# One fused adaLN block on one core: contractions over 448 rows as 64-row pairs of two tiles, stage 1 evicted by tile pairs, LayerNorm 2's scale and shift on transposed blocks

## The chip, the core and the metric

The kernel runs on one NeuronCore of one Trainium2 chip. The core has five engines with instruction queues of their own: TensorE (PE, matmuls; its weight loads are listed as PEld), VectorE (DVE), ScalarE (ACT), GpSimd (POOL) and SyncE (SP), which here issues most transfers. The metric is device time in microseconds (us) of the launch, the median of several runs; lower is better.

## The reference

One block with two branches on x of 2048 x 448 (bf16), a linear attention with learned softmax features (16 heads of 28) and a gated MLP with a spatial mixing matrix of 2048 x 2048. `silu(c) @ w_mod` gives two shifts, two scales and two gates.

```
sa, ca, ga, sb, cb, gb = split(silu(c) @ w_mod)
h = layernorm(x) * (1 + ca) + sa
q, k, v = heads(h @ wqkv)
phi(t) = concat(softmax(t @ w_phi), softmax(-t @ w_phi))
kv = phi(k)^T v;  z = sum(phi(k));  o = phi(q) kv / (phi(q) z + 1e-6)
x = x + ga * (o @ wo)
h = layernorm(x) * (1 + cb) + sb
z1, z2 = split(gelu(h @ w_in));  z2 = layernorm(z2)
g = w_sp @ z2 + b_sp[:, None]
x = x + gb * ((z1 * g) @ w_out)
```

Here w_in is 448 x 1792, so z1 and z2 have 896 columns.

## The kernel before

The 2048 rows are 16 tiles of 128. The work is a set of small steps (nested functions of `fast_path`), each of which issues a few instructions for one tile, one pair of tiles or one block. One string, `ORDER`, lists the steps; a word is `step:arguments/engine@bank`. The loop over its words is the program: every engine runs its instructions in that order, and each instruction waits only for the data and buffers that it needs. DMAs stand in the queue of the engine after the slash (`/Y` is SP); the transposes through the DMA (`T1`, `T2`, `T3`, and `W` for w_sp) always stand in SP's queue.

The steps fall into three stages.

Stage 1 (k, v and features). `l1s`, `l1e`, `l1r`, `l1a` normalise x without scale and shift; these are folded into the weights. Tiles are transposed in 4 blocks of 112 of the 448 columns (`hT`). Per tile `kM` and `vM` (L893, L901) are 4 matmuls each; `kE`, `kF` take exp of k and of -k on ACT, `vC` copies v on ACT, `kS` sums and `kR` inverts on DVE, `kP` multiplies on DVE or POOL, `kA` (L922) adds 8 narrow matmuls into the sum kv.

Stage 2 (q, attention output, LayerNorm 2, z). `qM` (L945) makes q for four tiles in one half of the heads. Per tile `nM` (L973) makes numerators and denominators, 8 matmuls of 120 columns over 128 rows against a block-diagonal kv; `nX`, `nC`, `nS` make the weights of the two softmax halves, `nT` (L989, DVE, 896 elements) applies them, `nA` (L995) adds the halves into `opad`. `T2` transposes it to `oT`. `wM` (L1005) multiplies by wo with 4 matmuls, for some tiles with a fifth that adds x (L1003). `wR` (L1010, L1012) adds the residual and sums the rows, `wQ` sums the squares, `l2R` and `l2r` make mean and inverse deviation, `l2a` (L1038) normalises into `xpad`, and `T3` transposes it to `hT`, in the same 4 blocks of 112 rows; a row of ones beside them carries the shift. Scale and shift of LayerNorm 2 are folded into w_in by `SCw` (L797 to L801), `SHw` (L784) and `FB` (L790). `zM` (L1049) makes z2 for a tile with 8 matmuls of 448 columns, `zG` applies GELU, `zQ`, `zR`, `zW`, `zN` normalise to `f_z2n`. `yM` (L1078) makes a 128-column block of z1, transposed, for four tiles with 4 matmuls of 512 columns, and `yG` applies GELU.

Stage 3 (mixing and output). The product with w_sp is done with 7 block products for each 2 x 2 (`P`, L1124, 8 matmuls of 512 columns each; `tT` and `sS` make the sums that they need), with column block 6 apart (`gM`, L1145). `d` and `x` add b_sp and multiply by z1; `oM` (L1159) multiplies by w_out with 7 matmuls, `oE` (L1162) adds x, `oD` stores.

PSUM has three slots of two banks (A0 to A2) and two of one (B0, B1) in stages 1 and 2.

```
for word in ORDER.split():
    ...
        STEPS[nm](*[int(v) for v in arg.split(",") if v], **kw)
```

Of the kernel before, what the change touches and what calls it, by code (L numbers as in the profile page):

```python
# [1266 lines left out]
```

## Time and profile before

| | us |
|---|---|
| median of 3 runs | 249.34 |
| lowest and highest | 248.21, 249.86 |
| the profiled execution, whole | 249.99 |
| its span in the trace | 248.1 |
| stage 1 and what leads to it, to the first nM | 54.0 |
| stage 2, to the first matmul of the mixing that runs in a row | 84.4 |
| mixing and output, to the last matmul | 105.3 |
| last residual add and store | 4.4 |

The busy shares of the 40 slices of the span, from the page:

```profile
PE   8999999989999899999999999999999999999992
DVE  5689999978998889687571997798976363645552
ACT  2488898846999697867897100000000000000000
POOL 4768997500587468988508000521129610124430
PEclk9999999999999999999999999999999999999999
```

Each digit is the busy share of an engine in one 6.2 us slice, in tenths; PEclk is the clock that TensorE was granted, full throughout. A matmul's row shows its whole passage (352 ns for 448 columns), though the next one follows long before its end; so PE's busy share says that it always has something under way, not that it is at its peak. ACT ends after slice 23, where the mixing begins.

### The profile page before, as it was taken

To read this page: it belongs to the slowest core of one execution; us is meant where nothing else is said; L and a number is where in the kernel's file an instruction comes from. 1 tells how busy PE (TensorE), PEld (TensorE's weight loads), DVE (VectorE), ACT (ScalarE), POOL (GpSimd) and SP (SyncE) were. 2 spreads that over 40 slices of the span, in tenths; PEclk is the share of its full clock that TensorE was granted. 3 is DMA by queue.
4 is the path that set the end of the run, shared out by engine and by line. 5 is a ranking of instruction groups with operands and counts; after the bars stand their busy time and mean duration, and the time that the engine had idled before them with its cause. 6 is when DMAs were issued, how large, how long until landed. Compare 5 with 4: busy or idle time off the path is not lost.

```text
span 248.1 us, 4186 instructions
## 1 busy us (share of the span) xinstructions
...
## 2 busy tenths in 40 slices
PE   8999999989999899999999999999999999999992
...
DVE  5689999978998889687571997798976363645552
ACT  2488898846999697867897100000000000000000
POOL 4768997500587468988508000521129610124430
PEclk9999999999999999999999999999999999999999
...
GB/s 176 265 245 106 188 86 161 208 160 144 45 79 114 137 121 145 157 154 180 190 171 0 152 176 186 0 1 0 3 0 37 0 0 3 56 0 37 21 95 65
DMA packets 68207, 25.22 MB, mean 102 GB/s; under 512 B 58129, under 2 KB 67602, under 8 KB 68178
## 3 DMA queue, kind: packets, MB, share of 16 engines
...
q8 instruction: 14, 0.23, 0.4%
q14 instruction: 15, 0.12, 0.2%
...
## 4 chain that ended last, share of the span: by engine, by line
PE 59%; DVE 13%; POOL 12%; issue 8%; ACT 3%; DMA 3%; POOLq 0%; DVEq 0%
PE g_ps L1124 29%; PE o_ps L1159 9%; PE z_ps L1049 5%; PE g_ps L1145 5%; DVE f_ksum L907 4%; PE z_ps L1078 4%; DMA f_hT<-f_xpad 3%; DVE f_st L859 3%; PE warm_ps L729 3%; POOL f_xpad L1038 2%; POOL f_ar L995 2%; POOL f_phik L914 1%; DVE f_phik L914 1%; POOL f_zv L1035 1%; DVE f_kr L911 1%
## 5 line engine op out<-in xcount | busy, mean ns | idle before, releaser
L1133 DVE TENSOR_TENSOR f_zb<-g_ps,f_zb 128x512 f32<-128x512 f32 (+1 forms) x31 | 20.5, 670 | 17.1 <-PE g_ps L1124 16.7
L1124 PEld LDWEIGHTS <-f_z2n 128*128 128x128 bf16 x192 | 18.8, 98 | 22.7 <-issue 0.3
L1140 POOL TENSOR_TENSOR f_z1T<-f_zb,f_z1T 128x512 bf16<-128x512 f32 (+1 forms) x11 | 11.9, 1101 | 33.6 <-DVE f_zb L1133 33.6
L1078 PE MATMUL z_ps<-f_hT,f_ar 112*128 112x512 bf16 x112 | 26.1, 379 | 1.3 <-DMA f_hT<-f_xpad 1.3
L1049 PE MATMUL z_ps<-f_ar,f_hT 112*128 112x448 bf16 (+1 forms) x128 | 26.7, 352 | 0.0
L1140 POOL TENSOR_TENSOR f_z1T<-f_Sx,f_z1T 128x512 bf16<-128x512 f32 x6 | 8.0, 1333 | 39.3 <-DVE f_Sx L1133 39.3
L1159 PE MATMUL o_ps<-f_wout,f_z1T 128*128 128x448 bf16 x112 | 22.5, 352 | 0.0
L1124 PE MATMUL g_ps<-f_ar 128*128 128x512 bf16 x94 | 22.2, 379 | 0.1
L1081 ACT ACTIVATE f_z1T<-z_ps,f_zb 128x512 bf16<-128x512 f32 x28 | 18.2, 684 | 6.7 <-PE z_ps L1078 6.5
L950 ACT ACTIVATE f_Eq<-q_ps 128x1024 bf16<-128x1024 f32 x16 | 16.4, 1033 | 5.8 <-PE q_ps L945 5.8
L1049 PEld LDWEIGHTS <-f_hT 112*128 112x128 bf16 (+1 forms) x128 | 12.2, 97 | 11.6
L1078 PEld LDWEIGHTS <-f_ar 112*128 112x128 bf16 x112 | 10.9, 98 | 14.1 <-issue 1.6
L989 DVE TENSOR_TENSOR f_ar<-num,f_w 128x896 bf16<-128x896 f32 x16 | 17.0, 1086 | 0.4
L896 ACT ACTIVATE f_E<-k_ps 128x448 bf16<-128x448 f32 x32 | 15.7, 563 | 3.1 <-PE k_ps L893 1.6
L907 DVE TENSOR_REDUCE f_ksum<-f_E 128x32 f32<-128x896 bf16 x16 | 16.7, 1060 | 0.2 <-ACT f_E L896 0.2
L1053 ACT ACTIVATE f_zb<-z_ps 128x896 bf16<-128x896 f32 x16 | 14.6, 913 | 4.2 <-PE z_ps L1049 3.8
L1124 PE MATMUL g_ps<-f_Eq,f_z2n 128*128 128x512 bf16 x70 | 16.2, 379 | 0.1
L1159 PEld LDWEIGHTS <-f_z1T 128*128 128x128 bf16 x112 | 11.0, 98 | 10.7
L1162 DVE TENSOR_TENSOR f_xpad<-o_ps,f_x 128x448 bf16<-128x448 f32 x16 | 9.9, 622 | 8.0 <-PE o_ps L1159 7.9
L945 PE MATMUL q_ps<-f_hT,f_Wq 113*128 113x512 bf16 (+1 forms) x64 | 15.0, 378 | 0.4 <-ACT f_Eq L950 0.4
L1124 PEld LDWEIGHTS <-f_ar 128*128 128x128 bf16 x96 | 9.4, 98 | 11.1 <-DVE f_ar L1102 0.2
L893 PE MATMUL k_ps<-f_Wk,f_hT 113*128 113x448 bf16 (+1 forms) x64 | 14.2, 352 | 0.2 <-ACT f_E L896 0.2
...
## 6 DMA issues: line engine op xcount, KB each, us to landing
...
```

Of the source, the lines that this page charges most:

```text
L896: nc.scalar.activation(out=Er[i % NR][:, :, s, :], in_=ps["k" + str(i)][:, 0, 0:D].rearrange("p (a e) -> p a e", a=8), func=ACT.Exp, scale ...
L907: nc.vector.tensor_reduce(out=ksum[:, i], in_=Er[i % NR][:].rearrange("p a s (f h) -> p (a s) h f", h=2), axis=AX.X, op=ALU.add)
L945: nc.tensor.matmul(t[:, u, :], lhsT=Wq[0:KR[m], m, cc * P:(cc + 1) * P], rhs=hT[0:KR[m], 4 * st:4 * st + 4, m, :], start=(m == 0), stop=(m ...
L950: nc.scalar.activation(out=Eq[st // 2][:, 2 * c2:2 * c2 + 2, s, (st % 2) * 512:(st % 2 + 1) * 512], in_=ps["q" + str(n)][:], func=ACT.Exp, ...
L989: nc.vector.tensor_tensor(out=tr[i % 2][:], in0=numv(i)[:, :, :, 0:DH], in1=wr[i // 2 % 2][:, i % 2].unsqueeze(3).to_broadcast([P, 2, H, D ...
L1049: nc.tensor.matmul(t[:, hf, 0:D], lhsT=hT[0:KR[m], i, m, :], rhs=win_s[0:KR[m], m, FH + hf * D:FH + (hf + 1) * D], start=(m == 0), stop=(m ...
L1078: nc.tensor.matmul(t[:, 0, :], lhsT=win_s[0:CB, m, fc * P:(fc + 1) * P], rhs=hT[0:CB, 4 * st:4 * st + 4, m, :], start=(m == 0), stop=(m == ...
L1081: nc.scalar.activation(out=stage_b()["z1T"][:, fc, st * 512:(st + 1) * 512], in_=ps["y%d_%d" % (st, fc)][:, 0, :], func=ACT.Gelu_apprx_tan ...
L1124: nc.tensor.matmul(g, lhsT=sta[:, m, :], rhs=mov[:, m, :], start=(m == 0 and i in (1, 6, 7)), stop=(m == 7), skip_group_check=True)
L1133: nc.vector.tensor_tensor(out=o, in0=x, in1=y, op=ALU.add)
L1140: eng.tensor_tensor(out=z, in0=T[r][:, c0:c1], in1=z, op=ALU.mult)
L1159: nc.tensor.matmul(ps["o" + str(t)][:, 0, 0:D], lhsT=later["z1T"][:, FO[n], t * P:(t + 1) * P], rhs=wout_s[:, FO[n], :], start=(n == 0), s ...
```

## The change

Pairs of half height. 448 is 7 x 64. Where a contraction ran over 4 blocks of 112 rows, it now runs over 7 blocks of 64. Tile 2j stands on rows 0 to 63 and tile 2j + 1 on rows 64 to 127 of one 128-row block, and the weights (wo, w_in) are in SBUF twice, once on each half. A matmul of the lower half is issued right behind that of the upper half, into another PSUM bank. So `wM`, `zM` and `yM` handle two tiles (`yM` eight), and the transposes `T2` and `T3` move 7 blocks a pair instead of 8. `nM` splits its 128-row contraction in the same way into two of 56 rows: 16 matmuls of 60 columns instead of 8 of 120.

```diff
+    def zM(j, sa, sb):
+        t = [bank(sa), bank(sb)]
...
+        for hf in range(2):
+            for cc in range(7):
+                for a in range(2):
+                    nc.tensor.matmul(t[a][:, hf, 0:D], lhsT=hT2[64 * a:64 * a + 64, j, cc, :], rhs=W2[64 * a:64 * a + 64, cc, hf * D:(hf + 1) * D],
+                                     start=(cc == 0), stop=(cc == 6))
-        for m in range(KC):
-            nc.tensor.matmul(t[:, 0, :], lhsT=win_s[0:CB, m, fc * P:(fc + 1) * P], rhs=hT[0:CB, 4 * st:4 * st + 4, m, :], start=(m == 0), stop=(m == KC - 1))
+        for cc in range(7):
+            for a in range(2):
+                nc.tensor.matmul(t[:, a, :], lhsT=W1[64 * a:64 * a + 64, cc, fc * P:(fc + 1) * P], rhs=hT2[64 * a:64 * a + 64, 4 * u:4 * u + 4, cc, :],
+                                 start=(cc == 0), stop=(cc == 6))
-        for cc in range(KC):
-            nc.tensor.matmul(t[:, 0, 0:D], lhsT=oT[0:CB, i % 4, cc, :], rhs=wo_s[0:CB, cc, :], start=(cc == 0 and not with_x), stop=(cc == KC - 1))
+        for cc in range(7):
+            for a in range(2):
+                nc.tensor.matmul(t[:, a, 0:D], lhsT=oT[64 * a:64 * a + 64, j % 2, cc, :], rhs=wo2[64 * a:64 * a + 64, cc, :], start=(cc == 0), stop=(cc == 6))
-                nc.tensor.matmul(t[:, s, cc * 120:(cc + 1) * 120], lhsT=E[:, cc, s, o:o + P],
-                                 rhs=KVbd[:, s, cc, :, :].rearrange("p h d -> p (h d)"), start=True, stop=True)
+                for a in range(2):
+                    nc.tensor.matmul(t[:, a, (s * 4 + cc) * 60:(s * 4 + cc + 1) * 60], lhsT=E[64 * a:64 * a + 56, cc, s, o:o + P],
+                                     rhs=KVd[64 * a:64 * a + 56, s, cc, :, :].rearrange("p h d -> p (h d)"), start=True, stop=True)
```

LayerNorm 2's scale and shift are no longer in w_in. `SCw`, `SHw` and `FB` go; the four columns are made by `cB` and `eB`, and a new step `hS` multiplies and adds in place on a transposed block, for two pairs at a time (256 columns), 28 instructions on ACT, DVE and POOL.

```diff
+    def hS(cc, a, b, eng):
+        v = hT2[:, a:b, cc, :]
+        if eng is nc.scalar:
+            nc.scalar.activation(out=v, in_=v, func=ACT.Identity, scale=colB[:, 1, cc:cc + 1], bias=colB[:, 0, cc:cc + 1])
+        else:
+            eng.tensor_scalar(out=v, in0=v, scalar1=colB[:, 1, cc:cc + 1], scalar2=colB[:, 0, cc:cc + 1], op0=ALU.mult, op1=ALU.add)
```

Stage 1 by pairs. k and v of two tiles go to the two banks of one slot, so that `kE`, `kF`, `vC`, `kS` and `kR` are one instruction for two tiles. `yG` covers 1024 columns instead of 512, `nA` two tiles instead of one. `wR` is always on DVE with the residual added there.

```diff
-        nc.vector.tensor_reduce(out=ksum[:, i], in_=Er[i % NR][:].rearrange("p a s (f h) -> p (a s) h f", h=2), axis=AX.X, op=ALU.add)
+        nc.vector.tensor_reduce(out=ksum[:, 2 * j:2 * j + 2], in_=Er[j % 3].rearrange("p t a s (f h) -> p (t a s) h f", h=2), axis=AX.X, op=ALU.add)
-        eng.tensor_tensor(out=opad[:, i % NO, :, 0:CB], in0=v[0], in1=v[1], op=ALU.add)
+        eng.tensor_tensor(out=opad[:, j % 2].rearrange("p c t e -> p c t e"), in0=v[0], in1=v[1], op=ALU.add)
```

The moments of both later LayerNorms are split into single steps `mA` to `mF`, which the order may place on DVE or POOL one by one. PSUM is one tile of eight banks with four slots of two, and most SBUF buffers lie in one arena.

All steps stand in a new order. Of the string, one line of each:

```diff
-nX:0 nX:1 qF:3 nC:0 csB@B0 W:0,1 ld:win1/Y nC:1 nS:0 ccB@B1 nT:0 qM:4@A2 qE:4 nA:0/V nT:1 ecB nA:1/V wos:3/V qM:5@A1 nM:2@A0 qF:4 esB nX:2 nM:3@A2 nX:3
+nX:1/S nC:1 nD:0 ld:w21/S du:2@B7 qM:3@A3 nI:0 nW:0 nT:0 qE:2 nT:1 qF:2 nM:2@A1 qF:3 nM:3@A2 nX:2/S qM:4@A0 wos:4,7/G nX:3/S nC:3 nA:0/G W:0,7 nC:2 nD:1 nI:1
```

Two places of the order. First POOL's queue in stage 2, ahead of the first normalised tile of LayerNorm 2. Before (f_m and f_v are mean and inverse deviation, f_cb the scale, f_ar the arena):

```order
L799 TENSOR_SCALAR f_ar<-f_ar,f_cb_82 112x896
L995 TENSOR_TENSOR f_ar<-f_ar 128x4x112
L1025 TENSOR_SCALAR f_m_89<-f_s_87 128x2
L1026 TENSOR_TENSOR f_sq<-f_m_89 128x2
L1028 TENSOR_SCALAR f_v_90<-f_s_88 128x2
L1029 TENSOR_TENSOR f_v_90<-f_v_90,f_sq 128x2
L1032 TENSOR_SCALAR f_v_90<-f_v_90 128x2
L1035 TENSOR_TENSOR f_v_90<-f_v_90,f_mhalf 128x2
L1038 TENSOR_SCALAR f_xpad<-f_x,f_m_89,f_v_90 128x4x112
```

and with the change, from the mean of tiles 0 and 1 on:

```order
L1016 TENSOR_SCALAR f_m_82<-f_s_80 128x2
L1036 TENSOR_TENSOR f_v_83<-f_v_83,f_mhalf 128x2
L1039 TENSOR_SCALAR f_xpad<-f_x,f_m_82,f_v_83 128x7x64 x2
L1020 TENSOR_TENSOR f_sq<-f_m_82 128x2
L988 TENSOR_TENSOR f_ar<-f_ar 128x2x7x64
L1028 TENSOR_TENSOR f_v_83<-f_v_83,f_sq 128x2
L1032 TENSOR_SCALAR f_v_83<-f_v_83 128x2
```

The power and the two normalisations of tiles 2 and 3 now come first; between the mean and the deviation of tiles 0 and 1 stands an add of a whole pair into `opad`, and the power and the normalisation of tiles 0 and 1 follow behind the last row.

Second SP's queue at the same time, around the first transposes of stage 2. Before:

```order
L644 DMA f_ar<-in_B_w_in_dram 112x2x1792
L875 DMA_TRANSPOSE f_ar<-f_ar 128x4x128 x2
L875 DMA_TRANSPOSE f_ar<-f_ar 128x8x128 x2
L1043 DMA_TRANSPOSE f_hT<-f_xpad 128x4x128
L875 DMA_TRANSPOSE f_ar<-f_ar 128x8x128
```

and with the change:

```order
L670 DMA f_ar<-in_w_mod_dram 112x4x960
L991 DMA_TRANSPOSE f_ar<-f_ar 128x7x128 x2
L675 DMA f_ar<-in_B_w_in_dram 64x7x896
L991 DMA_TRANSPOSE f_ar<-f_ar 128x7x128
L1043 DMA_TRANSPOSE f_hT<-f_xpad 128x7x128 x2
```

The first transpose of LayerNorm 2 (L1043) came as a single tile behind two single tiles and two pairs of `opad`; now it comes as two pairs in a row behind five pairs, with two loads of weights among those.

More of the change, by code (lines that the diff above doesn't have):

```diff
@@ L637, in fast_path @@
-    later = {}
+    crr = [persist.tile([P, 2, 2, 2, 8], F32, name=f"f_cr{r}") for r in range(2)]
+    dnr = [persist.tile([P, 4, 8], F32, name=f"f_dn{r}") for r in range(2)]
+    wr = [persist.tile([P, 4, 2, 8], F32, name=f"f_w{r}") for r in range(2)]
+    g_rep1 = persist.tile([P, D], BF, name="f_g_rep")
+    bmask = persist.tile([CB, 4], BF, name="f_bmask")
+    one1 = persist.tile([1, 1], BF, name="f_one1")
+    e = persist.tile([DC, KC], F32, name="f_e")
+    scol = persist.tile([DC, KC], BF, name="f_scol")
@@ L639, in fast_path @@
+    zero = carve(51072, 512)
+    c_row = carve(51584, D)[0:1]
+    ot = [xflat[:, 512 * r:512 * r + D] for r in range(4)]
+    g_rep = [g_rep0, g_rep1[:]]
     xv = A_x[0].rearrange("(n p) d -> p n d", p=P)
@@ L786, in FB, with ecA @@
-    def FB(slot):
-        t = ps["FB"] = bank(slot, "fb_ps")
-        for fc in range(FC):
-            for m in range(KC):
-                nc.tensor.matmul(t[:, 0, fc:fc + 1], lhsT=win_s[0:CB, m, fc * P:(fc + 1) * P], rhs=Gb[0:CB, m, CB:CB + 1], start=(m == 0), stop=(m == KC - 1))
-    def FBc(eng):
-        copy_on(eng, zb1[:, 0:FC], ps["FB"][:, 0, 0:FC])
+    def ecA():
+        nc.vector.tensor_scalar(out=ca1[0:CB, :], in0=ps["ccA"][0:CB, 0, 0:KC], scalar1=1.0, scalar2=None, op0=ALU.add)
@@ L886, in XE @@
         copy_on(eng, hT[:, i], ps["X" + str(i)][:, 0:512].rearrange("p (k t) -> p k t", k=KC))
-    KR = [C1, CB, CB, CB]
-    def kM(i, slot):
-        t = ps["k" + str(i)] = bank(slot, "k_ps")
-        for m in range(KC):
-            nc.tensor.matmul(t[:, 0, 0:D], lhsT=hT[0:KR[m], i, m, :], rhs=Wk[0:KR[m], m, :], start=(m == 0), stop=(m == KC - 1))
-    def kE(i, s):
-        nc.scalar.activation(out=Er[i % NR][:, :, s, :], in_=ps["k" + str(i)][:, 0, 0:D].rearrange("p (a e) -> p a e", a=8), func=ACT.Exp, scale=1.0 - 2.0 * s)
```

659 lines of the change are left out of this document (322 added, 337 removed).

## The prediction

> **What bounds the kernel now.** I read the stretches first, then what TensorE (PE) waited for, then the chain that ended last in order of time. The stretches, cut where a stage begins (first columns: stretch and its length in us, then busy us of each engine):
>
> ```profile
> 0.00:12.20 12.20, 10.68 (x128) 8.46 (x129) 7.25 (x27) 4.37 (x9) 7.12 (x26) 1.00 0.93 220
> 12.20:54.00 41.80, 40.86 (x357) 23.16 (x356) 39.69 (x84) 33.40 (x65) 29.34 (x33) 1.00 0.74 167
> 54.00:74.60 20.60, 20.07 (x209) 12.53 (x209) 18.11 (x49) 17.35 (x40) 8.69 (x17) 1.00 0.42 94
> 74.60:81.50 6.90, 5.61 (x42) 3.18 (x40) 6.22 (x17) 5.89 (x16) 5.45 (x11) 1.00 0.66 111
> 81.50:110.00 28.50, 28.22 (x165) 14.60 (x165) 22.80 (x60) 21.58 (x50) 21.49 (x44) 1.00 0.77 141
> 110.00:138.40 28.40, 28.10 (x138) 13.15 (x138) 16.93 (x39) 22.11 (x41) 15.17 (x29) 1.00 0.74 141
> 138.40:243.70 105.30, 104.75 (x491) 48.81 (x500) 71.95 (x102) 0.00 (x0) 29.89 (x19) 1.00 0.21 43
> ```
>
> and PE's longest single wait, for the first transposed block of LayerNorm 2 (us in total, times, the longest):
>
> ```profile
> PE z_ps L1078 <- DMA f_hT<-f_xpad: 1.3, 1, 1.3
> ```
>
> PE is full from 81.5 us on. Before that, in stage 1 (12.2 to 54) and in the ramp of stage 2 (54 to 81.5), VectorE (DVE) is nearly as full: 39.7 of 41.8 us, then 18.1 of 20.6 and 6.2 of 6.9. So an edit that takes work from PE is worth its whole size after 81.5, and before 81.5 only as much as DVE lets through.
>
> What a matmul costs PE is its pace in a run, not the 352 or 379 ns of its row. Pieces of the chain (start, us, what):
>
> ```profile
> 82.55 3.04 PE z_ps L1049 x16
> 87.11 0.85 PE num L973 x16
> 105.12 3.45 PE z_ps L1078 x16
> 233.03 10.61 PE o_ps L1159 x56
> 243.66 0.63 DVE f_xpad L1162
> ```
>
> and, from the timeline, a run of narrow ones:
>
> ```profile
> 45.16 0.62 PE L922 MATMUL kvacc<-f_vaug,f_phik 128*128 128x58 bf16 x16
> ```
>
> 448 columns cost 10.61/56 = 0.19 us, 512 columns 3.45/16 = 0.216, 120 columns 0.053. At 58 columns, (0.62 - 0.19)/15 = 0.029 us (0.19 is the tail of the last), the weight load included. Stage 3 is 336 products and 64 gate matmuls of 512 columns and 112 output matmuls of 448: 400 x 0.216 + 112 x 0.19 = 107.5 us without a gap, so back from its end at 243.6 it begins at 136.1.
>
> **What PE loses.** The rows of the matmuls that change or go:
>
> ```profile
> L1078 PE MATMUL z_ps<-f_hT,f_ar 112*128 112x512 bf16 x112 | 26.1, 379 | 1.3 <-DMA f_hT<-f_xpad 1.3
> L1049 PE MATMUL z_ps<-f_ar,f_hT 112*128 112x448 bf16 (+1 forms) x128 | 26.7, 352 | 0.0
> L1005 PE MATMUL x_ps<-f_ar 112*128 112x448 bf16 x64 | 14.1, 352 | 0.3 <-DVE f_x L1012 0.3
> L1003 PE MATMUL x_ps<-f_x,f_ident 128*128 128x448 bf16 x5 | 1.8, 351 | 0.0
> L784 PE MATMUL sh_ps<-f_ar,f_Gb 112*128 112x448 bf16 x8 | 1.8, 352 | 0.0
> L790 PE MATMUL fb_ps<-f_Gb,f_ar 112*128 112x1 bf16 x28 | 0.8, 163 | 0.0
> ```
>
> Contraction over 448 rows took 4 matmuls of 112; it becomes 7 steps of 64 rows, two tiles side by side, one in the upper and one in the lower half of the array. If the two run together, two tiles take 7 paces instead of 8. yM: 112 x 0.216 = 24.2 us becomes 98 pairs, 21.2: -3.0. zM: 128 x 0.19 = 24.3 becomes 112 pairs, 21.3: -3.0. wM: 69 x 0.19 = 13.1 (with the five that add x) becomes 56 pairs, 10.6: -2.5. The shift matmuls SHw (8 x 0.19) and FB (28 x 0.029) go: -2.3. nM: 128 matmuls of 120 columns (6.8 us) become 256 of 60; at 0.029 each if the issue sets the pace that is 7.4, together less: 0. Sum -10.8 us.
>
> No row of before shows two matmuls side by side. The bounds of a pair are one pace (0.19) and two (0.38). I take one: the halves share no rows, no weights and no PSUM bank, and nothing in the rows (weight loads are busy 14.6 of 28.5 us from 81.5 on) speaks for a queue between them. The Trainium skill ("TensorE: Matmul & The Clock Gate", Part 3) gives a pack of such matmuls the duration of one plus some 4 ns for each further tile; no run shows it yet, and by it 266 pairs of zM, yM and wM would cost 1.1 us more, an estimate from that page.
>
> Going from whole to half rows and back happens 16 times, by the order of the words: eight groups of pairs. The nearest row is the step from the one-row matmuls of c to the transposes:
>
> ```profile
> 6.34 0.23 PE L740 MATMUL ct_ps<-f_one,f_c_row 1*112 1x1 bf16 x1
> 6.50 0.19 PEld L823 LDWEIGHTS <-f_wk_raw 112*112 112x112 bf16 x2
> ```
>
> 0.16 us from start to start, hence 0 to 2.6 us in all. Fifteen of the sixteen lie ahead of the first zM, where PE has to wait anyway (below), so I take 0 and keep 2.6 for the range. The Trainium skill ("TensorEngine Tiling (Array Packing)", Tiling Modes, Key Properties) says that changing the mode drains TensorE; that speaks against this change. The row allows it at up to 0.16 us a time, and the sum by it would lose those 2.6 us where nothing hides them.
>
> **What the other engines gain and lose.** The rows (line, engine, operation, out<-in, count, busy us and mean ns of one, then idle us before it):
>
> ```profile
> L989 DVE TENSOR_TENSOR f_ar<-num,f_w 128x896 bf16<-128x896 f32 x16 | 17.0, 1086 | 0.4
> L907 DVE TENSOR_REDUCE f_ksum<-f_E 128x32 f32<-128x896 bf16 x16 | 16.7, 1060 | 0.2 <-ACT f_E L896 0.2
> L911 DVE RECIPROCAL f_kr<-f_ksum 128x32 bf16<-128x32 f32 x16 | 5.0, 334 | 0.3
> L1012 DVE SCALAR_TENSOR_TENSOR f_x<-x_ps,f_x 128x448 bf16<-128x448 f32 x11 | 6.8, 617 | 1.2 <-PE x_ps L1005 1.0
> L995 POOL TENSOR_TENSOR f_ar<-f_ar 128x448 bf16<-128x448 bf16 x4 | 4.1, 1036 | 14.1 <-DVE f_ar L989 14.1
> L1035 POOL TENSOR_TENSOR f_v<-f_v,f_mhalf 128x2 f32<-128x2 f32 x8 | 5.8, 728 | 0.5
> L1038 POOL TENSOR_SCALAR f_xpad<-f_x,f_m,f_v 128x448 bf16<-128x448 bf16 x9 | 6.5, 726 | 0.7
> L1053 ACT ACTIVATE f_zb<-z_ps 128x896 bf16<-128x896 f32 x16 | 14.6, 913 | 4.2 <-PE z_ps L1049 3.8 <-ACT f_z1T L1081 0.3
> L950 ACT ACTIVATE f_Eq<-q_ps 128x1024 bf16<-128x1024 f32 x16 | 16.4, 1033 | 5.8 <-PE q_ps L945 5.8
> L1017 ACT ACTIVATE f_ar<-f_zb 128x896 bf16<-128x896 bf16 x9 | 8.6, 950 | 0.2
> L980 DVE TENSOR_TENSOR f_cr<-num,f_Sx 128x32 f32<-128x32 f32 x16 | 2.6, 188 | 2.7 <-ACT f_Sx L977 2.7
> L984 DVE TENSOR_TENSOR f_dn<-f_cr 128x32 f32<-128x32 f32 x8 | 1.5, 192 | 0.2
> L985 DVE RECIPROCAL f_dn<-f_dn 128x32 f32<-128x32 f32 x8 | 2.8, 353 | 0.3
> L986 DVE TENSOR_TENSOR f_w<-f_Sx,f_dn 128x64 f32<-128x64 f32 x8 | 1.8, 225 | 0.3
> L995 DVE TENSOR_TENSOR f_ar<-f_ar 128x448 bf16<-128x448 bf16 x12 | 4.6, 396 | 0.1
> L1017 ACT ACTIVATE f_ar<-f_x 128x448 bf16<-128x448 bf16 x12 | 6.9, 577 | 1.8 <-DVE f_x L1012 1.7
> L1032 POOL TENSOR_SCALAR f_v<-f_v 128x2 f32<-128x2 f32 x6 | 1.5, 254 | 0.5
> ```
>
> The transposes into f_hT, from the issue to the landing:
>
> ```profile
> DMA to landing us min/median/max: 2.5/3.4/4.8
> ```
>
> Stage 1. The sums and reciprocals by pairs are 8 + 8 instructions instead of 16 + 16. The reduction keeps its elements, so it gains at most a start-up each; a reciprocal of 64 costs between 0.33 and 0.67, so that gain is 0 to 2.7 us; I take 1.3. Two more phik products go from DVE to GpSimd (POOL), which hides them (29.3 busy of 41.8). One q matmul group of 8 x 0.216 = 1.7 us leaves stage 1 for stage 2. DVE and PE both get some 2.5 us shorter: nM starts at 51.5 instead of 54.
>
> The ramp. PE's work from nM to the first zM is 16 nM x 0.43, five qM x 1.73, five wM pairs x 1.33 and 0.8 for the columns: 23 us, 26 with the switches: ready at 77.5. But zM now needs three things more than in before: both tiles of a pair, two pairs transposed (one scale and shift covers both), and the scale and shift itself. By DVE's order the residual add of tile 0 (L1012 of before) stands behind ten products of 0.19, eight of the wide nT at 1.05, four groups of sum, reciprocal and product (0.77), one add of a pair (under 2 x 0.4) and three residual adds: 1.9 + 8.4 + 3.1 + 0.7 + 2.1 = 16.2 us of DVE, 17 with its gaps: 68.5. Behind that POOL's order has a power (0.73), two normalisations (1.45), a wide opad add (2 x 1.04 = 2.1, it now covers a pair), some five small moments (0.25 each), another power and two normalisations: 7.7 us: 76. Then the transpose lands (3.4, with 2.5 and 4.8 as ends), and seven scale-and-shift instructions of 256 elements on ACT and POOL: between a 32-wide row's 0.19 and a 448-wide one's 0.73 each, four in a row, say 2. The first zM starts at 81.5 to 82, 4 us after PE is ready. That is the stall that takes the place of removed work. What of the -10.8 lies ahead of 82 (SHw, FB, half of wM, some 3.5 us) is therefore lost in it.
>
> The dense stretch. From the first zM to stage 3: 8 zM pairs x 2.66, 14 yM x 1.51 and 3 wM x 1.33 = 46.4 us of PE. ACT has beside it 16 GELU of 0.91, 12 of 1024 elements at 1.03, 10 squares of 0.95, five narrow squares of 0.58 and three scale-and-shifts of 0.4, some 40.6 us: just not the bound, and I add 2 us for PE waiting on a bank that ACT still reads. DVE has 39 us or so. Stage 3 then begins at 82 + 48.4 = 130.4 instead of 136.1: -5.7 us.
>
> Stage 3 keeps its matmuls and its tail (0.63 us of DVE and an output transfer); its rows of before leave PE no idle time, and DVE has 72 of 105 us. The second copies of w_in and wo (64 rows twice, some 2 MB) run on queues at a share of 0.74 before 54 us and 0.42 after: 0, with the landing's 4.8 as its end.
>
> **Sum.** -5.7 us from the profiled execution's 249.99 us (its span 248.1 and 1.9 around it) is 244.3. That execution is 0.65 us above the median of the runs, 249.34, so the forecast is 243.6 us.
>
> **Rivals.** (a) The ramp isn't late: the wait on the first block stays what it is in before, 1.3 us, since DVE and POOL have slack that their order lets them use. Then all of -10.8 counts but the 0.2 to 1 of new waits: 239 us. For it: DVE has 2.5 of 20.6 us idle in the ramp. Against it: the chain above is in order. (b) The gain is eaten: landing at 4.8 for T2 and T3 (+2.8), and either the switches in the open (+2.6) or ACT as the bound of the dense stretch: some 248.7 us. For it: DMA at 0.77 and ACT at 22 of 28 us there. (c) The pairs don't run side by side, which is also the case that the change doesn't do what it says. 266 more paces: 168 x 0.19 + 98 x 0.216 = 53 us, less the 4 us that the ramp would hide: 292 us. It decides as soon as a pair costs over 0.021 us more than one matmul (5.7/266). For it: no row shows an overlap. Against it: nothing that the halves share.
>
> **How the numbers follow.** My forecast, pairs together and a late ramp, 241 to 246.8 us: 0.48. (a), 237 to 241: 0.20. (b), 246 to 252.5: 0.20. (c) or a good part of it, above 252.5: 0.12. A measurement tells about 1% from no change, that is 246.9 and 251.8. Faster holds the forecast, (a) but for nothing, and little of (b): 0.67; same is most of (b): 0.18; slower the end of (b) and (c): 0.15. The range 237 to 252.5 leaves out (c) and the low end of (a).
>
> **What would show it.** Right: zM and yM pairs spaced 0.19 and 0.216 us a pair; PE idle some 4 us before the first zM, put down to DMA or to the scale and shift; stage 3 as long as before and starting near 130. Wrong: pairs spaced over 0.21 us; a ramp with no idle time; ACT without a gap between 82 and 130; idle PE in stage 3 on a late piece of w_sp.

## The result and the profile after

The changed kernel takes 273.48 us (median of 4 runs, 270.73 to 273.84) against 249.31 (4 runs beside them): a ratio of 1.0952, 95% interval 1.087 to 1.1033. It is slower, and outside the range of the prediction. The profiled execution took 273.8 us, its span is 272.0. In this document a ratio leaves out executions over 1.5% above the fastest of their kernel while the median holds them (e2, and e9, one of whose four took 400.24 us); e3 and e12, where that leaves one execution each (273.67 and 302.54 us), have no ratio, and the traces of e2, e3 and e12 are of such a longer execution, so their stages serve for orders of size only.

The busy shares of the 40 slices, from the page of the changed kernel (6.8 us each):

```profile
PE   7899997877798699999999949999759999999993
DVE  4749999887989977574755998854996652755762
ACT  2557876625377549987985000000000000000000
POOL 4458998864268827784889650760993175032300
PEclk9869999989599569999999988999968999999998
```

Two things are new. Counted from 1, TensorE has holes in slices 7 to 14 (the end of stage 1 and the ramp, which is the part of stage 2 from the first nM to the first zM), at 24 and at 29 to 30 (stage 3). And the granted clock, full throughout before, falls around these holes. The stretches show where the time is; first the kernel before, cut at its first nM, at the first matmul of the mixing (3.0 us ahead of the cut in the table of the kernel before) and at the last matmul (stretch, length, busy us of PE, PEld, DVE, ACT and POOL, then the clock, the DMA share and GB/s):

```profile
53.97:135.36 81.39, 79.29 (x538) 42.36 (x538) 61.37 (x158) 65.09 (x142) 49.55 (x97) 1.00 0.67 128
135.36:243.63 108.27, 107.49 (x503) 49.93 (x511) 74.64 (x105) 1.87 (x4) 31.14 (x21) 1.00 0.22 45
```

and the changed kernel, with stage 2 cut once more at the first zM:

```profile
13.06:58.27 45.21, 40.21 (x327) 22.78 (x326) 39.76 (x63) 29.29 (x38) 37.68 (x39) 0.95 0.79 165
58.27:94.50 36.23, 28.96 (x400) 14.51 (x401) 32.17 (x86) 20.78 (x48) 20.31 (x32) 0.79 0.61 120
94.50:146.25 51.75, 50.28 (x462) 31.39 (x463) 34.37 (x97) 42.54 (x80) 35.64 (x64) 0.95 0.85 148
146.25:267.33 121.08, 112.69 (x515) 50.95 (x513) 82.63 (x100) 1.94 (x2) 54.01 (x28) 0.96 0.16 33
```

Stage 1 ends at 58.3 instead of 54.0 (+4.3); stage 2 takes 36.2 + 51.8 = 88.0 instead of 81.4 (+6.6); stage 3 takes 121.1 instead of 108.3 (+12.8); the tail behind the last matmul takes 4.7 instead of 4.5 us. That is the 23.9 us between the spans. Stage 3, in which no matmul changed, loses most, and GpSimd has 54.0 us of work there where it had 31.1.

The pairs do what they should. From the timeline of TensorE (start, us, what):

```profile
78.05 1.91 PE L930 MATMUL f_psum<-f_hT,f_ar 113*128 113x512 bf16 x8
79.89 1.50 PE L997 MATMUL f_psum<-f_ar 64*128 64x448 bf16 x14
81.22 0.39 PE L962 MATMUL f_psum<-f_ar,f_Eq 56*128 56x60 bf16 x16
...
101.12 2.84 PE L1059 MATMUL f_psum<-f_ar,f_hT 64*128 64x448 bf16 x28
103.76 1.52 PE L997 MATMUL f_psum<-f_ar 64*128 64x448 bf16 x14
...
113.47 9.39 PE L1075 MATMUL f_psum<-f_hT,f_ar 64*128 64x512 bf16 x84
```

The 28 matmuls of zM take 103.76 - 101.12 = 2.64 us, that is 14 paces of 0.19: a pair costs one pace. Going to half rows costs 79.89 - 78.05 - 8 x 0.216 = 0.11 us. The nM behind that wM uses half rows too (56), and its start shows no step (81.22 - 79.89 = 1.33 = 7 x 0.19). The way back to whole rows shows where the last yM meets stage 3:

```profile
138.59 7.73 PE L1075 MATMUL f_psum<-f_hT,f_ar 64*128 64x512 bf16 x70 [0.52 <-ACT f_ar L1063]
146.25 3.63 PE L1122 MATMUL f_psum<-f_wsp,f_ar 128*128 128x512 bf16 x16
```

It costs 146.25 - 138.59 - 35 x 0.216 = 0.10 us.

The two holes of stage 3, each as TensorE, VectorE and GpSimd have it:

```profile
149.74 4.64 POOL L1105 TENSOR_TENSOR f_ar<-f_ar 128x1024 bf16<-128x1024 bf16 x2
149.80 2.60 DVE L1105 TENSOR_TENSOR f_ar<-f_ar 128x1024 bf16<-128x1024 bf16 x1 [0.83 <-POOL f_ar L1069]
152.32 4.20 DVE L1112 TENSOR_TENSOR f_ar<-f_ar,f_wsp 128x4096 bf16<-128x4096 bf16 x1
160.54 5.75 PE L1122 MATMUL f_psum<-f_ar 128*128 128x512 bf16 x18 [3.75 <-DVE f_ar L1105]
...
190.31 7.93 POOL L1112 TENSOR_TENSOR f_ar<-f_hT 128x4096 bf16<-128x4096 bf16 x1 [6.88 <-PE f_psum L1122]
192.79 5.99 DVE L1136 TENSOR_TENSOR f_ar<-f_ar 128x512 bf16<-128x512 f32 x1
200.04 3.57 PE L1122 MATMUL f_psum<-f_wsp,f_ar 128*128 128x512 bf16 x8 [4.63 <-DVE f_ar L1130]
```

VectorE's instructions with two inputs in SBUF stretch as long as a large GpSimd instruction runs beside them: tT 2.60 us, sS:0,2 4.20, x 5.99. Elsewhere in this trace the same forms take 0.68, 2.28 and 0.68 us:

```profile
148.29 0.68 DVE L1105 TENSOR_TENSOR f_ar<-f_ar 128x1024 bf16<-128x1024 bf16 x1
166.57 2.28 DVE L1112 TENSOR_TENSOR f_Eq<-f_wsp,f_Eq 128x4096 bf16<-128x4096 bf16 x1
183.96 0.68 DVE L1136 TENSOR_TENSOR f_ar<-f_ar 128x512 bf16<-128x512 f32 x1
```

What TensorE waits for stands behind them in VectorE's queue. And after the second wait the first 8 matmuls take 3.57 us where 1.89 is usual: half clock. The Trainium skill ("GPSIMD Engine Reference", 8. Key points) says that GpSimd shares its SBUF interfaces with VectorE and contends with VectorE's instructions that have two SBUF inputs; these rows agree.

### The profile page after: what moved, and what is told of

The parts are those of the page before. It is cut to its first block, busy times and chain, and to the rows that moved or that the text cites. A ratio compares the mean times of both kernels' runs of the same rounds, so it can differ in the third digit from the quotient of the medians.

```text
span 272.0 us, 4796 instructions
## 1 busy us (share of the span) xinstructions
PE 242.9 (89%) x1848; PEld 128.8 (47%) x1848; DVE 197.6 (73%) x369; ACT 99.4 (37%) x176; POOL 153.0 (56%) x183
## 4 chain that ended last, share of the span: by engine, by line
PE 49%; DVE 18%; DMA 9%; POOL 8%; issue 7%; ACT 4%; SPq 2%; POOLq 0%; DVEq 0%; ACTq 0%
PE f_psum L1122 26%; PE f_psum L1156 8%; PE f_psum L1075 5%; DMA f_x<-in_A_x_dram 4%; DMA f_hT<-f_xpad 3%; PE f_psum L1141 3%; DVE f_ar L983 3%; POOL f_xpad L855 3%; PE f_psum L930 2%; PE f_psum L997 2%; DVE f_ar L1136 2%; DVE f_x L1000 2%; DVE f_ar L1130 2%; DMA f_ar<-in_c_dram 2%; ACT f_ar L1063 1%
## 5 line engine op out<-in xcount | busy, mean ns | idle before, releaser
L1122 PEld LDWEIGHTS <-f_ar 128*128 128x128 bf16 x288 | 28.6, 100 | 44.7 <-issue 9.4
L1122 PE MATMUL f_psum<-f_ar 128*128 128x512 bf16 x144 | 34.7, 393 | 3.8 <-DVE f_ar L1105 3.8
L1130 DVE TENSOR_TENSOR f_ar<-f_psum,f_ar 128x512 f32<-128x512 f32 (+1 forms) x31 | 20.4, 668 | 16.5 <-PE f_psum L1122 16.2
L879 PE MATMUL f_psum<-f_ar,f_hT 112*128 112x448 bf16 (+1 forms) x128 | 28.2, 366 | 1.7 <-DMA f_hT<-f_xpad 1.7
L1059 PE MATMUL f_psum<-f_ar,f_hT 64*128 64x448 bf16 x224 | 25.7, 377 | 1.7 <-ACT f_hT L1048 0.8
L1075 PE MATMUL f_psum<-f_hT,f_ar 64*128 64x512 bf16 x196 | 22.2, 376 | 0.5 <-ACT f_ar L1063 0.5
L1156 PE MATMUL f_psum<-f_wout,f_ar 128*128 128x448 bf16 x112 | 22.7, 352 | 0.0
L930 PE MATMUL f_psum<-f_hT,f_ar 113*128 113x512 bf16 (+1 forms) x64 | 18.4, 437 | 0.4 <-DVE f_ar L983 0.4
L935 ACT ACTIVATE f_Eq<-f_psum 128x1024 bf16<-128x1024 f32 x16 | 15.7, 1024 | 7.3 <-PE f_psum L930 6.7
L901 POOL TENSOR_TENSOR f_ar<-f_ar 128x896 bf16<-128x896 bf16 x9 | 15.6, 1750 | 2.7 <-DVE f_ar L898 1.6
L988 POOL TENSOR_TENSOR f_ar<-f_ar 128x896 bf16<-128x896 bf16 x5 | 9.4, 1879 | 12.7 <-DVE f_ar L983 10.2
L1063 ACT ACTIVATE f_ar<-f_psum 128x896 bf16<-128x896 f32 x16 | 14.5, 909 | 5.2 <-PE f_psum L1059 3.6
L888 ACT ACTIVATE f_ar<-f_psum 128x896 bf16<-128x896 f32 x16 | 14.2, 927 | 5.3 <-PE f_psum L879 3.3
## 6 DMA issues: line engine op xcount, KB each, us to landing
f_x<-in_A_x_dram SPq DMA_DIRECT2D x2, 448.0 KB, 11.2
```

The costliest lines, as they stand in the source:

```text
L879: nc.tensor.matmul(t, lhsT=hT[0:KR[m], i, m, :], rhs=W[0:KR[m], m, 0:D], start=(m == 0), stop=(m == KC - 1))
L930: nc.tensor.matmul(t[:, u, :], lhsT=Wq[0:KR[m], m, cc * P:(cc + 1) * P], rhs=hT[0:KR[m], 4 * st:4 * st + 4, m, :], start=(m == 0), stop=(m ...
L935: nc.scalar.activation(out=Eq[st // 2][:, 2 * c2:2 * c2 + 2, s, (st % 2) * 512:(st % 2 + 1) * 512], in_=ps["q" + str(n)], func=ACT.Exp, sc ...
L1059: nc.tensor.matmul(t[a][:, hf, 0:D], lhsT=hT2[64 * a:64 * a + 64, j, cc, :], rhs=W2[64 * a:64 * a + 64, cc, hf * D:(hf + 1) * D], start=(c ...
L1063: nc.scalar.activation(out=z2g[i % NZ].rearrange("p (a d) -> p a d", a=2), in_=ps["z" + str(i)][:, :, 0:D], func=ACT.Gelu_apprx_tanh, accu ...
L1075: nc.tensor.matmul(t[:, a, :], lhsT=W1[64 * a:64 * a + 64, cc, fc * P:(fc + 1) * P], rhs=hT2[64 * a:64 * a + 64, 4 * u:4 * u + 4, cc, :], ...
```

## The experiments

Two theories stood at the start. A: the pairs give what was forecast, and the loss is what the new order makes, by waits, by stretched instructions and by half clock after the waits. B: pairs or layout cost by themselves. Edits are shown as words of the order; / names the engine (V, S, G, Y for VectorE, ScalarE, GpSimd, SyncE). The lengths are those of the profiled execution: when nM starts, the ramp from there to the first zM, the dense stretch from there to stage 3, and stage 3.

| run | median us | ratio to before, 95% | nM | ramp | dense | stage 3 |
|---|---|---|---|---|---|---|
| changed kernel | 273.48 | 1.0952 (1.087 to 1.1033) | 58.3 | 36.2 | 51.8 | 121.1 |
| e1 | 267.65 | 1.0791 (1.0722 to 1.086) | 59.3 | 35.5 | 52.3 | 113.5 |
| e2 | 266.50 | 1.0601 (1.0526 to 1.0675) | 63.4 | 34.9 | 51.7 | 113.2 |
| e3 | 281.57 | none | 61.9 | 36.7 | 51.8 | 124.6 |
| e4 | 270.84 | 1.0892 (1.0836 to 1.0948) | 56.8 | 35.0 | 51.6 | 120.4 |
| e5 | 259.37 | 1.0422 (1.0387 to 1.0458) | 56.2 | 35.4 | 51.5 | 110.4 |
| e6 | 272.05 | 1.0942 (1.0883 to 1.1002) | 59.4 | 36.6 | 52.2 | 117.2 |
| e7 | 271.81 | 1.0936 (1.0914 to 1.0958) | 60.3 | 35.2 | 50.8 | 120.8 |
| e8 | 263.62 | 1.0596 (1.0563 to 1.0629) | 60.2 | 36.2 | 52.0 | 110.4 |
| e9 | 256.25 | 1.0276 (1.0196 to 1.0356) | 54.4 | 31.9 | 49.7 | 110.4 |
| e10 | 269.52 | 1.0803 (1.0735 to 1.0871) | 56.5 | 33.4 | 63.3 | 110.4 |
| e11 | 266.41 | 1.0711 (1.0641 to 1.078) | 54.8 | 33.4 | 61.2 | 110.4 |
| e12 | 308.52 | none | 56.5 | 35.8 | 101.0 | not used |
| e13 | 255.73 | 1.0269 (1.0214 to 1.0323) | 55.2 | 34.7 | 51.0 | 109.0 |
| e14 | 275.92 | 1.1079 (1.1005 to 1.1153) | 61.3 | 35.5 | 52.5 | 120.6 |

**e1, stage 3 in the order of before.** From `tT:1,2` on, the words of stage 3 as before has them, with the slots of the new PSUM tile:

```diff
-tT:2,2/G tT:1,1/V ... P:0,0,1 ... P:0,1,1 ... gM:1@B7 ... gM:0@B6 ... P:0,0,6 ... P:0,1,6
+tT:1,1/V ... P:0,0,1 ... P:0,1,1 ... gM:1@B7 ... P:0,1,6 ... gM:0@B6 ... P:0,0,6 P:0,1,5
-sS:1,1,0,8/G
+sS:1,1,0,8/V
```

> The changed kernel with stage 3 alone put into the sequence, and on the engines, of the kernel before; the pairs, the tile layout and everything ahead of stage 3 stay as changed. Theory A (the pairs give what was forecast; the loss is waits that the new order makes, and a half TensorE clock after each of them): stage 3 takes 107 to 111 us instead of 121.3, its two idle stretches of 3.75 and 4.63 us go, the granted clock stays 1.0 there, and the time is 259 to 264 us. Theory B (paired matmuls, or the new layout in memory, make stage 3 slower by themselves): stage 3 stays above 117 us and the time above 269.

Between the two: stage 3 fell by 7.6 us to 113.5 and its clock was 1.0, but three waits came up (1.16, 1.93 and 2.07 us), and stage 1 was a microsecond longer, so stage 3 missed its range by 2.5 us and the time by 3.7. Without the waits stage 3 is 108.3, as in before. The old order doesn't fit the new layout wholly: T1b, which `tT:1` writes, now lies on W1, so it must follow the last yM.

**e2, six steps to VectorE, order kept.**

```diff
-tT:1,2/G tT:2,2/G ... tT:4,0/G ... tT:3,2/G ... tT:4,2/G ... sS:1,1,0,8/G
+tT:1,2/V tT:2,2/V ... tT:4,0/V ... tT:3,2/V ... tT:4,2/V ... sS:1,1,0,8/V
```

> The changed kernel in its own order; only six large SBUF steps of stage 3 (four of tT's five on POOL and one more of them, and sS:1,1) are issued to VectorE instead of GpSimd. If the stalls come from VectorE's instructions being stretched by large GpSimd instructions beside them (4.20 us where 2.29 is usual, 5.99 where 0.68 is): the first idle stretch shrinks from 3.75 to under 1.5 us, the second (4.63) goes, with the half clock behind both: 262 to 266 us, and no VectorE row of stage 3 stands over 2.7 us. If it is the sequence on VectorE (what stands ahead of tT:2,0) and not the stretching: the first stall stays over 3 us or grows, and the time stays within 3 us of 273.5.

The first wait shrank from 3.75 to 1.27 us as the stretching demands, the second from 4.63 only to 1.98, because sS:1,1 itself now stood in VectorE's queue. No instruction of VectorE takes over 2.7 us in that stage 3, as expected. VectorE did six more steps and its busy time in stage 3 fell, from 82.6 to 75.2 us. So stretching makes most of the two stalls, the queue the rest.

**e8, both.** The six steps, and two places:

```diff
-P:0,0,6 ... P:0,1,6 d:0,1,3
+P:0,1,6 d:0,1,3 P:0,0,6
-P:0,2,5 sS:1,1,0,8/G ... d:0,2,2
+P:0,2,5 ... d:0,2,2 sS:1,1,0,8/V
```

> The changed kernel with stage 3 alone edited: the six SBUF steps on VectorE as in the run before, and two places in the sequence: P:0,1,6, whose operands come first, ahead of P:0,0,6, and sS:1,1 behind d:0,2,2. Theory A: both idle stretches go (under 0.5 us left), no half clock after 150 us, stage 3 107.5 to 109.5 us, time 259 to 263 us where stage 1 does not wait longer for its rows of x. If contention alone explained the loss, the two places change nothing against e2 (stage 3 113.2 us, with idle stretches of 1.27 and 1.98 us).

Stage 3 of that run:

```profile
148.41:258.77 110.36, 107.84 (x505) 49.95 (x513) 76.99 (x106) 1.94 (x2) 36.73 (x22) 1.00 0.18 36
```

10.7 us less than in the changed kernel, and 9.9 us less in the medians, with stages 1 and 2 untouched. A wait of 1.72 us was left, before P:0,0,5, so the expectation was missed by one microsecond; e13 took it away (109.0). This is the proof for stage 3: eight words of the order are worth 10 of its 12.8 us.

**e3 and e6, dummies against the half clock.** Matmuls on a zero tile (`du`) or the identity (`fi`), without readers, where TensorE waits. The edit of e6:

```diff
+du:12@B0 ... du:10@B7 kA:13@B6 ... du:15@B7 nM:0@A2 ... fi:34@A3 nX:6/S nM:7@A2 ... fi:50@A1 nA:4/G ... du:30@B2 P:0,0,6 ... du:38@B6 P:0,2,2
```

> The changed kernel with dummy matmuls on TensorE put where it waits (before X:0, kA:13, nM:0, in eight places of the ramp, and before P:0,0,6 and P:1,1,1), 1 to 4 us in each, no wait taken away. If the half clock follows a stretch of little TensorE work, the granted clock of the span rises from 0.928 to over 0.97, the waits keep their lengths, and the time falls by 7 to 14 us, to 259 to 266. If the half clock follows something else (the paired matmuls, for one), the clock stays at 0.92 to 0.94 and the time within 2 us of 273.5 or above it.

> The fill of before with twice the dummies in the ramp, and the last one in front of P:0,2,2, where the wait is; no wait is taken away. If the half clock follows from idle TensorE and costs its full share: granted clock over 0.97, the second idle stretch of stage 3 filled and its half clock (199 to 206 us) gone, time 262 to 268 us. If the waits of VectorE's queue set the ends anyway and the half clock lies mostly beside them: the clock rises as well, but the time stays at 269 to 274 us.

e3 missed its range (281.57 us, 8.1 above the changed kernel) and told little: its last fill stood behind P:0,2,2, which is what waits, and so only added 4 us, and its dummies of 32 columns left the ramp's clock at 0.83. In e6 the clock of the span rose to 0.970 and stage 3 ran at full clock:

```profile
59.37:96.00 36.63, 31.47 (x584) 19.13 (x583) 33.90 (x88) 20.45 (x48) 19.69 (x31) 0.86 0.67 119
148.16:265.32 117.16, 115.12 (x572) 56.49 (x581) 83.45 (x100) 1.94 (x2) 53.50 (x27) 1.00 0.17 34
```

Stage 3 gained 3.9 us by it (121.1 to 117.2), the ramp nothing, the median 1.4 us. So the half clock is 4 of stage 3's 12.8 us and waits are the rest. In the ramp the clock only rose from 0.79 to 0.86, so what it costs there isn't shown. What it costs stage 1 stays open too, for the later loads of x (below) blur that stage.

**e4, loads of stage 1.** The steps that use the moved gate weights, `gr:1` and `ge:1`, move behind them.

```diff
-ld:wmgb/Y ... ld:wmga/Y ... ld:x3/Y ... ld:x4/Y ... W:0,5 ... T1:14,16 ... W:0,4
+ld:x3/Y ... ld:x4/Y ld:wmgb/Y ld:wmga/Y ... T1:14,16 W:0,5 W:0,4
```

> The changed kernel with stage 1's transfers put as they were: the two gate weights after the rows of x in SP's queue (the two gr steps beside each other), and the transposed blocks 5 and 4 of the spatial weight after T1:14,16. Theory A: rows 4 to 7 of x land 2 us sooner, the wait of 1.5 us for the transposed tiles 14 and 15 goes, and the first nM starts 2 to 4 us earlier than 58.3; since the ramp is set by VectorE, 1 to 3 us of it arrive at the end: 270 to 273 us. If stage 1 is bound by what GpSimd has to do (37.7 of 45.3 us), or by the half clock of 11.5 to 18 us, the first nM stays within 1 us of 58.3 and the time within 1.5 us of 273.5.

nM came at 56.8, the time fell by 2.6 us, within the range of theory A; the wait for the last transposes only went from 1.52 to 1.35 us. The six runs with the order's late loads and no dummies (the changed kernel, e1, e2, e7, e8, e14) start nM at 58.3 to 63.4, with waits on those transposes of 1.7 to 5.8 us in all; the seven with early loads at 54.4 to 56.8. What is left to before's 54.0 isn't settled. In e4 the stage starts 1.0 us later than in before (13.21, 12.20) and takes 1.7 us longer:

```profile
13.21:56.75 43.54, 38.01 (x329) 21.51 (x327) 39.68 (x64) 29.24 (x39) 37.75 (x39) 1.00 0.82 165
```

TensorE is busy for 38.0 us instead of before's 40.9, VectorE for 39.7 as before, so TensorE's saving finds VectorE nearly full; VectorE's other 3.9 us (2.1 in before) weren't tested.

**e7, the columns of LayerNorm 2 early.**

```diff
-wQ:2/S ld:wmb/Y ... nT:8 cB:0@B7 nT:9 eB:0,0 ... T2:5 cB:1@B6 ... eB:1,0 ... hS:1,0,2/S nM:12@A0 nX:12/S nC:12 hS:0,0,2/S
+ld:w11/Y ld:wmb/Y ... qM:2@A1 cB:0@B7 KZ:1,0 eB:0,0 eB:0,1 ... nM:1@A0 cB:1@B6 nC:0 ... eB:1,0 eB:1,1 ... hS:1,0,2/S hS:0,0,2/S nM:12@A0
```

> The changed kernel with the ramp alone edited: cB and eB (the scale and shift columns of LayerNorm 2) at the end of stage 1, where TensorE waits, their weights loaded earlier, and hS:0 ahead of nX:12 on ScalarE. If the ramp is held by the chain eB:1,1 (90.5 us) to hS to the first zM: the wait of 1.81 us before wM:5 goes and the first zM comes 3 to 4 us after the first nM sooner than the 36.2 us of now, 32 to 33, and the time falls to 269 to 271. If VectorE's work in the ramp (32.2 of 36.2 us) holds it: the ramp shortens by 0 to 1.5 us and the time stays at 272 to 274.

The ramp shortened by 1.0 us and the wait before wM:5 went: the second case, VectorE. The 1.0 us alone would show little, for with its words untouched the ramp takes 34.9 to 36.2 us (e1, e2, e4, e8).

**e5, all order edits.** The edits of e4, e8 and e7, and one more:

```diff
-kA:14@B6 wos:2,4/V kA:15@B6
+nT:1 wos:2,4/V qF:2
```

> All order edits together, the pairs and the layout as changed: the loads early, stage 3's six SBUF steps on VectorE with P:0,1,6 ahead of P:0,0,6 and sS:1,1 behind d:0,2,2, the gate's wos:2,4 out of the way of KV, and the column forms of LayerNorm 2 (cB, eB) made at the end of stage 1. Theory A (only order and placement lose the time): first nM 54 to 56 us, ramp 32 to 34, dense stretch 51 to 52, stage 3 108 to 110, sum 252 to 257 us, still above before since the ramp is VectorE's and the pairs take nothing off it. Theory B (the pairs or the layout cost by themselves): the stretches do not come back to these lengths and the time stays above 262.

14.1 us of the 24.2 came back; against B, but ramp and stage 3 stayed 1.4 and 0.4 us above what A allowed, and the time 2.4.

**e9, half of nT.** On e5; one of the two feature signs is left out of nT, and nA adds the other to itself.

```diff
-in0=numv(i)[:, :, :, :, 0:DH],
+in0=numv(i)[:, :, 0, :, 0:DH],
-for s in range(2)]
+for s in (0, 0)]
```

> The kernel with all order edits, and nT (the attention's quotient, 14 of which stand in the ramp at 1.09 us on VectorE) made for one of the two feature signs only, so that nA adds that one to itself: half of that part of the result is left out. If VectorE's work holds the ramp (32.4 of 35.4 us): VectorE has some 7 us less to do there, the ramp falls to 28 to 31 us and the time to 252 to 255. If it is the chain of small steps and transfers from wQ:0 to the first zM, or TensorE's half clock: the ramp stays over 33 us and the time over 256.

Stage 2 of e5, then of e9:

```profile
56.17:142.99 86.82, 77.39 (x848) 43.95 (x845) 67.59 (x180) 63.11 (x127) 56.66 (x94) 0.90 0.73 131
54.44:136.01 81.57, 71.79 (x845) 40.27 (x844) 60.45 (x181) 63.26 (x127) 56.89 (x95) 0.98 0.80 143
```

VectorE has 7.1 us less in stage 2 than in e5 (67.6), and stage 2 takes 5.2 us less (86.8 to 81.6), 3.5 in the ramp and 1.8 behind it, where the clock is back. The ramp stopped at 31.9, above its range: other waits, of 1.6 to 1.7 us each, took over. How much of the gain came by way of the clock, which rose from 0.81 to 0.95 in the ramp, isn't separated. With VectorE relieved, TensorE is busy for 71.8 us of stage 2 at 0.98 clock, against 79.3 before. That fits the pairs' saving, though the shift matmuls that went are in it too.

**e10 and e11, the chain ahead of the first zM pulled forward,** both on e5; e11 has three of nA on VectorE besides.

```diff
-nM:15@A2 nM:14@A0 ... T2:5 ... T3:1 ... T3:0 nM:13@A1 ... zM:1,3@A2
+mE:0,0,2/G mF:0,0,2 l2a:2/V T3:1 ... l2a:0/G l2a:1/V T3:0 ... T2:5 ... zM:1,3@A2 gt nM:15@A0 nM:14@A1 ... nM:13@A2
```

e11:

```diff
-nA:3/G ... nA:2/G ... nA:5/G
+nA:3/V ... nA:2/V ... nA:5/V
```

> The kernel with all order edits, and in the ramp the chain to the first zM pulled ahead of what it waited behind: wQ:1 before qE:7, the moments of tiles 0 and 1 in one go on GpSimd, the transposes T3:0 and T3:1 ahead of the load of the gate weights, and zM:1 ahead of the attention of tiles 12 to 15. If that chain's places in the queues hold the first zM: it comes 3 to 5 us earlier after the first nM (30 to 32 instead of 35.4 us) and the time falls to 254 to 257. If VectorE's work holds stage 2 as a whole: the first zM comes earlier all the same, but the dense stretch grows by as much, and the time stays at 258 to 260.

> As the run before, and three additions of the attention (nA:2, nA:3, nA:5, 1.88 us each on GpSimd) on VectorE, where one takes 0.61. If GpSimd's large instructions stretch VectorE's small ones beside them (1.75 us where 0.22 is usual) by about what they would cost there: VectorE's busy time in the ramp stays within 1 us and the time falls by 0 to 2 us. If VectorE is the bound and is not stretched: 1.5 to 2 us slower than the run before.

e10 was a miss: the ramp shortened by 2 us, but attention of tiles 12 to 15 came late and the dense stretch grew by 11.8 us, 10 slower in all. e11 is 3.1 us faster than e10 (1.7 us of it in a stage 1 that the edit doesn't touch), and VectorE, with three more additions, was busy 28.91 us in the ramp instead of 30.31.

**e12, no pairs.** On e5, both matmuls of a pair of zM and yM read the same 64 rows, so the other half of those sums is left out.

```diff
-lhsT=hT2[64 * a:64 * a + 64, j, cc, :], rhs=W2[64 * a:64 * a + 64, cc, hf * D:(hf + 1) * D],
+lhsT=hT2[0:64, j, cc, :], rhs=W2[0:64, cc, hf * D:(hf + 1) * D],
```

> The kernel with all order edits, and both matmuls of each pair of zM and yM reading the lower 64 rows: the upper half of the sum is left out (the lower one is taken twice), the number of matmuls stays 420, but no two may run side by side. If the pairs run side by side (2.84 us for 28 of zM): 112 x 0.19 + 98 x 0.216 = 42 us more on TensorE, the dense stretch 90 to 95 us, the time 298 to 303. If pairs do not overlap: the time stays at 259.

The dense stretch doubled, 51.5 to 101.0 us, and the shortest execution took 302.5. From the timeline of TensorE, 28 matmuls of zM as above:

```profile
92.97 9.49 PE L1060 MATMUL f_psum<-f_ar,f_hT 64*128 64x448 bf16 x25 [0.32 <-DVE f_x L1001]
...
119.10 5.46 PE L1060 MATMUL f_psum<-f_ar,f_hT 64*128 64x448 bf16 x28
```

5.46 us instead of 2.84. B's first half falls: pairs run side by side.

**e14, five nA on VectorE,** alone on the changed kernel (nA:0, 2, 3, 4 and 5).

```diff
-nA:0/G ... nA:3/G ... nA:2/G ... nA:5/G ... nA:4/G
+nA:0/V ... nA:3/V ... nA:2/V ... nA:5/V ... nA:4/V
```

> The changed kernel with one edit: the attention's five additions of GpSimd (nA) on VectorE. If large GpSimd instructions stretch VectorE's small ones beside them in the ramp by as much as the additions would cost VectorE itself (0.61 us each, 3 us together): VectorE's busy time in the ramp stays within 1 us of 32.2, the w rows (nW) fall from a mean of 490 ns to under 300, and the time falls by 1 to 3 us, to 270 to 272.5. If nothing is stretched: VectorE's busy time grows by 3 us and the time by 1 to 3 us.

VectorE's small instructions in the ramp (w, the sum, and the attention's additions; count, busy us, mean ns), of the changed kernel:

```profile
L979 DVE TENSOR_TENSOR f_w<-f_Sx,f_dn 128x64 f32<-128x64 f32 x7 | 3.4, 490 | 0.1
L973 DVE TENSOR_TENSOR f_dn<-f_cr 128x32 f32<-128x32 f32 x7 | 2.5, 350 | 0.1
```

and of e14:

```profile
L989 DVE TENSOR_TENSOR f_ar<-f_ar 128x896 bf16<-128x896 bf16 x6 | 3.6, 606 | 0.0
L980 DVE TENSOR_TENSOR f_w<-f_Sx,f_dn 128x64 f32<-128x64 f32 x7 | 1.6, 224 | 0.1
L974 DVE TENSOR_TENSOR f_dn<-f_cr 128x32 f32<-128x32 f32 x7 | 1.3, 187 | 0.1
```

The w rows halve, and VectorE's busy time is 31.7 us with 3.6 of additions where it was 32.2 with 0.6: the 3 us of additions that GpSimd had taken off VectorE came back there as stretching. The ramp fell by 0.7, which is within what it varies by untouched. The time didn't fall, against the expectation: nM came at 61.3, 3 us later than in the changed kernel, with 4.6 us of waits on transposes in a stage 1 that the edit doesn't touch.

**e13, the best of these.** e5 with nA on VectorE, P:0,1,5 ahead of P:0,0,5, kP:13 ahead of kP:14, and the load for cB earlier.

```diff
-nA:0/G ... nA:4/G ... kP:14/V kP:13/V ... W:3,3 P:0,1,5
+nA:0/V ... nA:4/V ... kP:13/V kP:14/V ... P:0,0,6 P:0,1,5
```

> The kernel with all order edits, and four more: the attention's five additions of GpSimd (nA, 1.88 us each) on VectorE, P:0,1,5 ahead of P:0,0,5, which waits, kP:13 ahead of kP:14, and the load for cB before the transposes of the spatial weight. If order and placement are what is lost: stage 3 108 to 109 us (the wait of 1.72 us gone), the ramp 33 to 34, the first nM at 54 to 55.5, and the time 252 to 256 us, which is still not below before. If VectorE is simply full in the ramp and not stretched: the ramp grows by 1 to 3 us and the time stays at 257 to 260.

```profile
13.57:55.22 41.65, 38.97 (x343) 22.35 (x342) 37.27 (x62) 29.19 (x38) 36.12 (x39) 0.99 0.90 194
55.22:89.89 34.67, 25.45 (x382) 12.65 (x382) 32.10 (x91) 20.49 (x48) 11.75 (x26) 0.90 0.56 106
89.89:140.92 51.03, 49.43 (x463) 27.16 (x463) 34.11 (x95) 42.59 (x81) 36.55 (x65) 0.97 0.87 149
140.92:249.96 109.04, 108.00 (x505) 50.00 (x513) 76.94 (x106) 1.94 (x2) 36.79 (x22) 1.00 0.18 37
```

255.73 us: 17.8 of the 24.2 us came back by order and placement alone. Stage 3 is within 0.8 us of before. Stage 2 still takes 85.7 us (81.4 before), with VectorE busy for 32.1 us of the ramp, and the ramp's 34.7 us lie 0.7 over the expected range. No run separates what is left there between the order and what pairs ask of the ramp (two tiles of each pair, and their scale and shift, before a first zM); that part of theory B stays open. No version ran below before.

## Why the prediction was wrong

**Pairs at one pace: right.** 0.19 and 0.216 us a pair, no 4 ns on top that the rows could show, and e12 gives the other side. Rival (c) falls, although the time lies above 252.5 us, where the prediction had put (c).

**The switches: right within bounds.** 0.11 us into half rows and 0.10 back, by one row each; for sixteen that is an estimate of 1.7 us of the 0 to 2.6 kept.

**"Stage 3 keeps its matmuls and its tail ... DVE has 72 of 105 us": the step that failed most.** It read from the row of before that TensorE has no idle time there, and carried that over to another order. It had no term for GpSimd's work in stage 3, and looked for trouble there only at a late piece of w_sp. The sum needed a term for what stands in VectorE's queue ahead of P's operands. Stage 3 measures 12.8 us more; e8's eight words return 10.7 of them, and e6 shows 3.9 of the 12.8 to be half clock.

**"nM starts at 51.5 instead of 54": failed by 6.8 us.** The second copies were costed at 0, and the new place of the gate weights in SP's queue had no term. They stand ahead of tiles 4 to 11 of x, whose loads land in 11.2 us instead of 8.8 (medians of two). Early loads return 1.5 us in the profile of e4. The rest: the 2.5 us were granted to both TensorE and VectorE, but VectorE's work in the stage stayed at 39.8 us, with 8.3 us more of GpSimd's beside it. Of VectorE's rows, kP in before (L914), then kP and the gate's product into wo (L947) in the changed kernel:

```profile
L914 DVE TENSOR_TENSOR f_phik<-f_E,f_kr 128x896 bf16<-128x896 bf16 x9 | 5.4, 614 | 0.1
L901 DVE TENSOR_TENSOR f_ar<-f_ar 128x896 bf16<-128x896 bf16 x7 | 5.9, 872 | 0.2
L947 DVE TENSOR_TENSOR f_ar<-f_ar 128x896 bf16<-128x896 bf16 x1 | 2.3, 2301 | 0.0
```

Seven kP cost more than nine did, and the product into wo, which now goes over 7 blocks of 448 columns instead of 4, had no term either; e5, which moves it out of the stage, has 37.6 us of VectorE there.

**The ramp: right in kind, wrong in size.** A late first zM on VectorE's chain was forecast, 30 us from nM, with some 4 us of TensorE idle in front of it; it is 36.2. The wait right in front of it is 0.78 us, on the scale and shift; eight others lie earlier in the ramp, 7.2 us in all nine and 4.9 of them on VectorE. Missing were VectorE's stretched rows (3.0 us by the two groups above), the order's placing of cB (a wait of 1.8 us, gone in e7) and the half clock (0.79 over the ramp), whose share isn't shown; e9 shows that VectorE's work holds the ramp.

**The dense stretch: 51.8 instead of 48.4.** TensorE's work was 46.4 in the sum; 5.4 us of the stretch run at half clock (0.95 over the whole, 2.6 us). Of the other 2.7 us the trace shows three waits, 1.1 us on ScalarE, for which 2 us stood, and 0.3 on GpSimd.

**Half clock: not in the sum at all.** Before, the clock was 1.00 throughout and the longest wait 1.3 us; the forecast put a 4 us wait into the ramp without asking what TensorE would do after it.
